# Batch 0's scores computed with tokens on partitions, raw weights loaded first, first weights used as two parts

## The chip, the cores and the metric

One core of a Trainium2 chip runs the kernel. The time is device microseconds; the kernel before takes 666.42 us, the median of 3 runs (665.63 to 666.83).

The engines are TensorE (PE, with its weight loads shown as PEld), VectorE (DVE), ScalarE (ACT), GpSimd (POOL, almost unused here), and SyncE (SP), whose queue issues all DMAs.

## The reference

Attention between 512 tokens and 32 states of each of 8 batches and 8 heads (dimension 64), in both directions, and then a feed-forward layer in which two products are multiplied elementwise.

```python
scores = scale * np.matmul(x, state.transpose(0, 1, 3, 2))
a = softmax(scores)                       # over the 32 states
xread = np.matmul(a, state)               # (B, H, 512, 64)
scores2 = scale * np.matmul(state, x.transpose(0, 1, 3, 2))
a2 = softmax(scores2)                     # over the 512 tokens
sread = np.matmul(a2, x)                  # (B, H, 32, 64)
x = concatenate([xread, sread], axis=2)   # to (4352, 512): heads side by side
return ((x @ w_a) * (x @ w_b)) @ w_out    # 512 -> 1536 -> 512
```

All arrays are float32. The weights come to the kernel as 64-bit floats in memory, seen as pairs of 32-bit words, and are rebuilt on the chip.

## The kernel before, in words

**Precision.** A float32 operand of the large products is kept as a high and a low part (`p_h`/`p_l`, `at_h`/`at_l`, `sd_h`/`sd_l` for batch 0's attention, `g_h`/`g_l`), and a product is three matmuls: high by high, high by low, low by high.

**Layer 1.** `x @ w` is not formed from xread. Since `xread @ w = a @ (state @ w)`, the kernel computes `state @ w` per batch and chunk of weights (`direct`, line 1298, for the first two chunks, from the float32 weights `wo6` to `wo9`), splits it into `p_h` and `p_l`, and multiplies by the attention weights `a`. The products land in the PSUM tiles `ab`; ACT and DVE multiply the two of them (`a_sb`), split the result (`g_h`, `g_l`), and layer 2 multiplies it by `w_out` (`wo0`, `wo1`, ...) into the PSUM tiles `acc`.

**The order of work.** The program only records its operations. `plan` (line 699) then sorts them, engine by engine, by estimated costs and by two tables of numbers, SHIFTS and RELEASES, and the loop at line 1798 issues them in that order. So nearly all instructions have the line 1798, each engine runs its list strictly in order, and a tile's name is what tells instructions apart. SP's DMAs are in one such list too; where one of them waits, those behind it wait.

**Start of the program.** `attend(0)` (line 1617) computes batch 0's attention in two halves of the heads, g = 0 and g = 1. For each half it computes the scores with states on the partitions (`scores`, 1111, tile `ms`), copies them to SBUF (`copied`, tile `p_raw`), turns them with four transposes so that tokens lie on the partitions (`scores_t`, 1138, tile `acc`), does the softmax over 32 states with DVE and ACT (`soft_t`, `exp`, `norm`, tile `s_p`), turns the result back (`back_t`, 1154) and splits it into `sd_h0` and `sd_l0`. The untransposed scores are also stored (`kept`), for the other direction later. `open_chunk(0)` (1674) loads the first chunk of weights in four raw blocks (`raw`, `raw`, `sd_h1`, `sd_l1` serve as rooms), each converted by `Whole` (960): ACT takes the upper words (`pre`, tile `t1`), DVE makes a rounded float32 from them (`wo6` and `wo7`) and a rest from the lower words (`t2`), and a last DVE addition joins the two. `direct` for batch 0 (`units[0].direct`, four calls of four matmuls, 64 rows by 32 columns of the array) follows each joined block.

80 matmuls on constants (`ab<-y`, line 894) run in the gaps of PE's list before its dense work.

After the start eight visits of one batch and two chunks each follow, then products over the remaining four chunks. The later batches' attention stands in between.

Of the kernel before, what the change touches and what calls it, by code (L numbers as in the profile page):

```python
# [10 lines left out]
F32 = mybir.dt.float32  # L11
# [9 lines left out]
P = 128  # L21
# [26 lines left out]
T0, PACE = 15e3, 1.12  # L48
STARTS = {}
# [246 lines left out]
class Engine:  # L296
# [557 lines left out]
def attn_moe(ctx, tc, xt, xn, sd, wl, w_out, out):  # L854
# [62 lines left out]
    class Conv:  # L917
# [6 lines left out]
        def load(self, place):  # L924
            self.raw = load64(self.src, place, self.runs)
            if not count[0]:
                u = rec.units[-1]
                u.serve, u.land, u.lat = u.serve + 1200, u.land + 900, u.lat + 2100
# [103 lines left out]
    def moving(c, f, g, hq):  # L1032
# [3 lines left out]
        if c:  # L1036
            return fw[c, g][rows, hq // 2]
# [803 lines left out]
```

## Time and profile before

| | before |
|---|---|
| median of 3 runs | 666.42 us |
| profiled execution | 665.46 us |
| its span | 663.3 us |
| DVE busy | 548.8 us, 83% |
| ACT busy | 383.0 us, 58% |
| DMA queue, share of 16 engines | 69.9% |

The times below come from the profiled execution. It is one of the executions of the program, and 0.96 us shorter than the median of the timed runs. A busy PE is not PE at its peak: an instruction's end is modelled, and two that overlap count once. What an engine waits for is inferred from its semaphores; the idle time stands in square brackets with the engine or DMA that ended it. In the timeline a row may hold several instructions of one kind. A float32 matmul (other than the split ones) shows as two in the trace.

### The profile page before, as it was taken

The numbers are of one execution on the slowest core, as the hardware profiler recorded it, in microseconds if no ns is written. First come the engines' busy times: TensorE is split into PE (matmuls) and PEld (weight loads), VectorE is DVE, ScalarE is ACT, GpSimd is POOL, SyncE is SP. The second block draws the span as 40 slices with busy tenths as digits, with TensorE's granted clock in tenths as the row PEclk, the third lists the DMA queues.
The fourth block names the chain that finished last, engine by engine and source line by source line (L and its number), as shares of the span: only waits on it lengthen the run. The fifth ranks groups of instructions, "written<-read, shape, count | busy, mean of one in ns | idle before, by whom it ended". The sixth has DMA issues, their size and how long they took to land.

```text
span 663.3 us, 12126 instructions
## 1 busy us (share of the span) xinstructions
PE 654.2 (99%) x4451; PEld 546.1 (82%) x4451; DVE 548.8 (83%) x1219; ACT 383.0 (58%) x707; POOL 0.7 (0%) x6
## 2 busy tenths in 40 slices
PE   7999999999999999999999999999999999999997
PEld 5566776776777778888888989898989989889996
DVE  5999989998877787878989978877777879877885
ACT  4677478699989976654545543534444444424442
POOL 0000000000000000000000000000000000000000
PEclk9999999999999999999999999999999999999999
DMA  8998579899989999866767764754426217168830
GB/s 304 354 366 332 222 253 344 301 317 356 351 300 393 339 327 351 328 189 198 257 235 219 246 232 124 249 168 159 155 101 169 102 48 223 65 182 188 233 97 33
DMA packets 75450, 155.98 MB, mean 235 GB/s; under 512 B 7040, under 2 KB 26240, under 8 KB 75392
## 3 DMA queue, kind: packets, MB, share of 16 engines
q1 hardware_dynamic: 75392, 155.22, 69.9%
q8 instruction: 35, 0.57, 0.4%
q14 instruction: 23, 0.19, 0.1%
HBM read 92.27 MB, written 62.91 MB: 234 GB/s over the span
## 4 chain that ended last, share of the span: by engine, by line
PE 93%; DVE 5%; issue 1%; DMA 0%; ACT 0%; DVEq 0%
PE ab L1798 44%; PE acc L1798 39%; PE ms L1798 10%; DVE t L1798 1%; DVE wo L1798 1%; DVE m L1798 1%; DVE s_p L1798 1%; DMA x<-xt 0%; DVE stg L1798 0%; DVE p_l L1798 0%; DVE x L1798 0%; ACT p_h L1798 0%; DVE a_sb L1798 0%; DVE u_c L1798 0%; DVE wq L1798 0%
## 5 line engine op out<-in xcount | busy, mean ns | idle before, releaser
L1798 PE MATMUL acc<-wo,g_h 128*128 128x256 f32 (+1 forms) x868 | 178.8, 316 | 0.3 <-DVE stg L1798 0.2
L1798 PEld LDWEIGHTS acc<-wo,g_h 128*128 128x128 f32 x868 | 135.4, 190 | 19.5 <-issue 3.4
L1798 PE MATMUL ab<-at_l,p_h 128*128 128x512 f32 x368 | 144.5, 393 | 0.0
L1798 PE MATMUL ab<-at_h,p_h 128*128 128x512 f32 x368 | 144.4, 397 | 0.0
L1798 PE MATMUL ab<-at_h,p_l 128*128 128x512 f32 x368 | 143.1, 391 | 0.0
L1798 PE MATMUL acc<-wo,g_l 128*128 128x256 f32 (+1 forms) x587 | 127.3, 308 | 0.2
L1798 PEld LDWEIGHTS acc<-wo,g_l 128*128 128x128 f32 x587 | 93.0, 190 | 11.5 <-issue 1.2
L1798 ACT CAST g_h<-a_sb 128x512 fp32r<-128x512 f32 (+1 forms) x104 | 64.0, 615 | 56.3 <-DVE a_sb L1798 26.6
L1798 PEld LDWEIGHTS ab<-at_h,p_h 128*128 128x128 f32 x368 | 69.1, 188 | 17.5 <-issue 2.9
L1798 PEld LDWEIGHTS ab<-at_h,p_l 128*128 128x128 f32 x368 | 69.1, 188 | 15.5 <-issue 0.8
L1798 PEld LDWEIGHTS ab<-at_l,p_h 128*128 128x128 f32 x368 | 69.3, 188 | 12.1 <-issue 0.8
L1798 DVE TENSOR_TENSOR g_h<-a_sb,g_h 128x512 fp32r<-128x512 f32 x68 | 46.7, 686 | 15.6 <-PE acc L1798 11.7
L1798 ACT COPY wq<-ab 128x512 f32<-128x512 f32 (+1 forms) x48 | 27.3, 569 | 43.5 <-PE ab L1798 43.3
L1798 DVE TENSOR_TENSOR wq<-ab,wq 128x512 f32<-128x512 f32 (+1 forms) x48 | 32.0, 666 | 21.9 <-PE ab L1798 18.9
L1798 ACT CAST p_h<-p_raw 128x1024 fp32r<-128x1024 f32 x32 | 33.7, 1054 | 21.7 <-PE ab L1798 20.5
L1798 DVE TENSOR_TENSOR p_l<-p_raw,p_h 128x1024 fp32r<-128x1024 f32 x32 | 39.0, 1218 | 1.5 <-ACT p_h L1798 1.4
L1798 DVE TENSOR_TENSOR stg<-acc,stg 128x256 f32<-128x256 f32 (+1 forms) x68 | 36.4, 552 | 3.6 <-PE acc L1798 2.6
L1798 ACT CAST g_l<-wq 128x384 fp32r<-128x384 f32 x46 | 23.6, 515 | 27.1 <-PE acc L1798 24.4
L1798 DVE TENSOR_TENSOR g_l<-wq,g_l 128x384 fp32r<-128x384 f32 x46 | 25.5, 555 | 14.5 <-PE acc L1798 9.8
L1798 ACT COPY p_raw<-ms 128x512 f32<-128x512 f32 x48 | 27.6, 591 | 10.7 <-PE ms L1798 8.5
L1798 DVE TENSOR_SCALAR t<-t 128x512 int32<-128x512 int32 x64 | 26.8, 420 | 5.3 <-ACT t L1798 5.0
L1798 DVE TENSOR_TENSOR a_sb<-ab,a_sb 128x512 f32<-128x512 f32 (+1 forms) x36 | 23.6, 657 | 6.7 <-PE ab L1798 5.3
(135 smaller groups left out, 1065.3 us busy)
## 6 DMA issues: line engine op xcount, KB each, us to landing
p_raw<-scr SPq DMA_DIRECT2D x32, 512.0 KB, 4.8
raw<-wl SPq DMA_DIRECT2D x20, 512.0 KB, 5.6
x<-xt SPq DMA_DIRECT2D x15, 576.0 KB, 7.1
out<-stg SPq DMA_DIRECT2D x33, 256.0 KB, 2.3
su<-wq SPq DMA_DIRECT2D x16, 512.0 KB, 5.8
scr<-sw_st SPq DMA_DIRECT2D x32, 256.0 KB, 4.6
scr<-p_raw SPq DMA_DIRECT2D x32, 256.0 KB, 4.8
x<-xn SPq DMA_DIRECT2D x16, 512.0 KB, 5.1
```

What stands on the lines that cost most here:

```text
L1798: getattr(obj, method)(*map(real, args), **{k: real(x) for k, x in kw.items()})
```

## The change

Four edits go together.

1. **Raw weights first.** The first raw block's load is issued before x's three loads (`head`), and its estimated landing in the planner is earlier.
2. **Scores straight.** For batch 0, `scores_t` no longer transposes. It multiplies with x as the stationary operand and the states as the moving one, so the scores come out with tokens on the partitions: for g = 0 eight matmuls with 64 columns moving, for g = 1 sixteen with 32. The scores with states on the partitions are still needed for `kept` and are computed after both halves.
3. **Two parts.** In the first chunk the rounded weight (`wo6`, `wo7`) and the rest (now in a `stg` tile instead of `t2`) are both multiplied and accumulated by `direct` for batch 0, and joined after it (`join`), for the other batches and for the stored copy.
4. **New tables.** SHIFTS and RELEASES have other numbers throughout, so that the whole order is sorted anew.

```diff
+XREL = 300.0
 SHIFTS = {
-    0: 961, 1: 522, 2: -345, 3: -1004, 4: 175, 5: 340, 6: 86993674, 7: 86992534, 8: -40, 9: 377, 10: -272, 11:
...
             if not count[0]:
                 u = rec.units[-1]
-                u.serve, u.land, u.lat = u.serve + 1200, u.land + 900, u.lat + 2100
+                u.serve, u.land, u.lat = u.serve + 600, u.land + 300, u.lat + 900
...
         def run(self):
             raw, t1 = self.raw, self.t1
-            o = self.parts()
-            t2 = proj.tile([P, 512], I32, name="t2")
+            o, t2 = self.parts()
...
-            nc.vector.tensor_tensor(out=f32(o), in0=f32(o), in1=f32(t2), op=ALU.add)
+            self.halves = o, f32(t2)
+
+        def join(self):
+            o, t2 = self.halves
+            nc.vector.tensor_tensor(out=f32(o), in0=f32(o), in1=t2, op=ALU.add)
...
-            return fw[c, i // 2][:, i % 2]
+            if c:
+                return fw[c, i // 2][:, i % 2], proj.tile([P, 512], I32, name="t2")
+            if i % 2 == 0:
+                rest_w[i // 2] = mlp.tile([P, 2, DM], F32, name="stg", bufs=4)
+            return fw[c, i // 2][:, i % 2], rest_w[i // 2][:, i % 2].bitcast(I32)
...
                     for h in range(2):
-                        nc.sync.dma_start(out=x[:, g, h], in_=xt[self.b, g, :, h])
+                        u = nc.sync.dma_start(out=x[:, g, h], in_=xt[self.b, g, :, h])
+                        u.rel = XREL
+                        u.touch.append(head.raw)
+                        u.acc.append((head.raw.tile, 0, False))
...
-            with rec.together(self.sp[g]):
+            with rec.together(self.sp[g]) as u:
                 for sb in range(4):
-                    nc.tensor.transpose(self.t[:, sb * P:(sb + 1) * P], self.s[g][:, sb * P:(sb + 1) * P], ident)
+                    x, o = slice(sb * P, (sb + 1) * P), self.t[:, sb * P:(sb + 1) * P]
+                    for h in range(2):
+                        if g == 0:
+                            nc.tensor.matmul(o.rearrange("p (i h n) -> p h i n", i=2, h=2)[:, h], lhsT=self.x[:, g, h, x],
+                                             rhs=self.st[:, g, h].rearrange("p (i n) -> p i n", i=2), start=True, stop=True)
+                        for hh in range(2) if g else ():
+                            j = place_of(g, 2 * h + hh)
+                            nc.tensor.matmul(o[:, j * NS:(j + 1) * NS], lhsT=self.x[:, g, h, x],
+                                             rhs=self.st[:, g, h, hh * NS:(hh + 1) * NS], start=True, stop=True)
...
-                            j, r = place_of(g, hq), moving(c, i, g, hq)
+                            j, parts = place_of(g, hq), (False, True) if psp else (False,)
...
+                            for k in parts:
+                                nc.tensor.matmul(ps[g][j * NS:(j + 1) * NS, x],
+                                                 lhsT=states_raw[hq % 2 * D:(hq % 2 + 1) * D, 2 * g + hq // 2, n],
+                                                 rhs=moving(c, i, g, hq, k), start=(i == fs[0] and not k),
+                                                 stop=(i == fs[-1] and k == parts[-1]))
...
         if a.wide:
             for g in range(NG):
-                a.scores(g)
-                a.copied(g)
                 a.scores_t(g, *where)
...
+            a.scores(0, 1)
+            for g in range(NG):
+                a.copied(g)
+                a.store(g)
             return
...
-            convert(whole(c, i), kind)
+            w = convert(whole(c, i) if c + i else head, kind)
             if c == 0:
                 units[0].direct(0, i // 2, i % 2, psp=ps_acc, tag="acc")
+            w.join()
...
+    head = whole(0, 0)
+    head.load(place(0, "early"))
+    count[0] += 1
```

How this moves instructions is seen in three places. The first is the start of PE's list, before, where `ms<-x` are the scores with states on the partitions and `acc<-ident,p_raw` their transposes:

```order
L1798 MATMUL ms<-x 32x512 x4
L1798 MATMUL ab<-y 128x256 x3
L1798 MATMUL acc<-ident,p_raw 128x128 x4
L1798 MATMUL ab<-y 128x256 x14
L1798 MATMUL ms<-x 32x512 x4
L1798 MATMUL ab<-y 128x256 x12
L1798 MATMUL acc<-ident,s_p 128x128 x4
L1798 MATMUL acc<-ident,p_raw 128x128 x4
```

and the same start of PE's list with the change, where `acc<-x` are the scores with tokens on the partitions:

```order
L1827 MATMUL ab<-y 128x256 x20
L1827 MATMUL acc<-x 128x2x32 x8
L1827 MATMUL ab<-y 128x256 x5
L1827 MATMUL ms<-x 32x512 x8
L1827 MATMUL ab<-y 128x256 x12
L1827 MATMUL acc<-ident,s_p 128x128 x4
L1827 MATMUL ab<-y 128x256
L1827 MATMUL acc<-x 128x32 x16
```

The transposes of scores are gone, 20 of the 80 warm-ups stand in front of all, and the scores of g = 1 come right behind the transposes of g = 0's result.

The second place is DVE's list from the second half's first reduction (g = 1) to its last multiplication, before (`wo7_210<-wo7_210,t2` are joins, `s_p_291` and `p_raw_267` belong to batch 1):

```order
L1798 TENSOR_REDUCE m1_238<-acc_196 128x16
L1798 TENSOR_TENSOR s_p_255<-acc_196,m1_238 128x512
L1798 TENSOR_SCALAR t2_257<-t1_234 128x512
L1798 TENSOR_SCALAR wo7_210<-t1_234 128x512
L1798 SCALAR_TENSOR_TENSOR t2_257<-sd_l1_144,t2_257 128x512
L1798 TENSOR_REDUCE m1_238<-s_p_255 128x16
L1798 TENSOR_TENSOR wo7_210<-wo7_210,t2_257 128x512
L1798 TENSOR_SCALAR m1_238<-m1_238 128x16
L1798 STREAM_TRANSPOSE s_p_291<-p_raw_267 128x512
L1798 RECIPROCAL m1_238<-m1_238 128x16
L1798 TENSOR_REDUCE m1_301<-s_p_291 128x16
L1798 TENSOR_TENSOR s_p_255<-s_p_255,m1_238 128x512
```

and with the change, behind the same first reduction and subtraction (`raw_143` is the first block of `w_out`, `sd_l1_152` the last raw block of the first chunk):

```order
L1827 TENSOR_SCALAR t2_292<-t1_265 128x512
L1827 TENSOR_SCALAR stg_228<-t1_223 128x512
L1827 TENSOR_SCALAR wo7_235<-t1_223 128x512
L1827 SCALAR_TENSOR_TENSOR stg_228<-sd_l1_152,stg_228 128x512
L1827 TENSOR_SCALAR t1_265<-t1_265 128x512
L1827 SCALAR_TENSOR_TENSOR t1_265<-raw_143,t1_265 128x512
L1827 TENSOR_REDUCE m1_286<-s_p_290 128x16
L1827 TENSOR_SCALAR raw_143<-t2_292 128x512
L1827 TENSOR_SCALAR m1_286<-m1_286 128x16
L1827 SCALAR_TENSOR_TENSOR wo0_295<-t1_265,raw_143 128x512
L1827 RECIPROCAL m1_286<-m1_286 128x16
L1827 TENSOR_TENSOR s_p_290<-s_p_290,m1_286 128x512
```

The joins and batch 1's operations have left this stretch, and five operations on `w_out` have come into it.

The third place is ACT's list around the exponential of g = 1, with the change (`t1_223` is the last raw block of the first chunk, `t1_265` and `t1_299` are the two first blocks of `w_out`, `s_p_290` the exponential):

```order
L1827 ACTIVATE t1_223<-sd_l1_152 128x512
L1827 ACTIVATE t1_265<-raw_143 128x512
L1827 CAST sd_l0_288<-acc_193 128x512
L1827 CAST wo0_295<-t2_292 128x512
L1827 ACTIVATE t1_299<-raw_232 128x512
L1827 ACTIVATE s_p_290<-s_p_290 128x512
```

Before, the exponential came right behind the conversion of the first chunk's last raw block, ahead of both blocks of `w_out`; now it stands behind both.

## Rows read from the trace of the kernel before

**Rows 1.** The page: span, and PE's busy time, share, instructions.

```profile
span 663.3 us, 12126 instructions
...
PE 654.2 (99%) x4451; PEld 546.1 (82%) x4451; DVE 548.8 (83%) x1219; ACT 383.0 (58%) x707; POOL 0.7 (0%) x6
```

**Rows 2.** Busy time by stage: stretch, length, then each engine's busy us.

```profile
0.00:26.00 26.00, 21.07 (x154) 14.79 (x155) 17.65 (x38) 11.62 (x21) 0.71 (x6) 1.00 0.93 323
```

**Rows 3.** Chain that ended last, 60 to 663.3 us, shares by line.

```profile
by line: PE ab L1798 46.4%; PE acc L1798 42.2%; PE ms L1798 9.2%; DVE stg L1798 0.3%; DVE p_l L1798 0.3%; DVE x L1798 0.2%; ACT p_h L1798 0.2%; issue 0.2%; DVE u_c L1798 0.1%; DVE wq L1798 0.1%; DVE xst L1798 0.1%; ACT u_c L1798 0.1%; DVEq
```

**Rows 4.** Timeline of DVE: start us, length us, engine, line, operation, tiles.

```profile
8.15 0.69 DVE L1798 TENSOR_REDUCE m<-acc 128x16 f32<-128x512 f32 x1 [8.15 <-PE acc L1798]
...
9.81 0.42 DVE L1798 TENSOR_SCALAR wo<-t 128x512 int32<-128x512 int32 x1
10.15 0.69 DVE L1798 SCALAR_TENSOR_TENSOR t<-raw,t 128x512 f32<-128x512 uint32 x1
...
10.75 0.68 DVE L1798 TENSOR_REDUCE m<-s_p 128x16 f32<-128x512 f32 x1
...
12.44 0.69 DVE L1798 TENSOR_TENSOR s_p<-s_p,m 128x512 f32<-128x512 f32 x1
...
16.79 0.69 DVE L1798 TENSOR_REDUCE m<-acc 128x16 f32<-128x512 f32 x1
...
22.01 1.28 DVE L1798 TENSOR_TENSOR s_p<-s_p,m 128x512 f32<-128x512 f32 x2
...
38.60 0.69 DVE L1798 TENSOR_TENSOR wo<-wo,t 128x512 f32<-128x512 f32 x1
```

**Rows 5.** Chain that ended last, 24 to 62 us: start us, us, what.

```profile
36.73 0.63 ACT g_h L1798
...
37.41 2.11 PE acc L1798 x8
```

**Rows 6.** Timeline of the first loads: an issue, and the end of PE's wait.

```profile
1.65 0.42 SPq L1798 DMA_DIRECT2D raw<-wl  x1
...
4.33 0.18 PEld L1798 LDWEIGHTS ms<-x 64*32 64x32 f32 x4 [0.50 <-DMA x<-xt]
```

**Rows 7.** Timeline of ACT: conversions of the raw blocks, with their waits.

```profile
8.56 0.67 ACT L1798 ACTIVATE t<-raw 128x512 f32<-128x512 f32 x1 [1.68 <-DMA raw<-wl]
...
11.73 0.67 ACT L1798 ACTIVATE t<-raw 128x512 f32<-128x512 f32 x1 [1.51 <-DMA raw<-wl]
...
15.92 0.68 ACT L1798 ACTIVATE t<-sd_l 128x512 f32<-128x512 f32 x1 [0.20 <-DMA sd_l<-wl]
```

**Rows 8.** Timeline of PE's weight loads, 128 by 128.

```profile
13.18 0.42 PEld L1798 LDWEIGHTS acc<-ident,s_p 128*128 128x128 f32 x4
...
25.84 0.19 PEld L1798 LDWEIGHTS ab<-sd_h,p_h 128*128 128x128 f32 x1 [0.95 <-ACT p_h L1798]
```

**Rows 9.** Timeline of PE: warm-ups, transposes, first weights, first dense matmul.

```profile
19.73 4.21 PE L1798 MATMUL ab<-y 128*128 128x256 f32 x33
...
23.78 0.60 PE L1798 MATMUL acc<-ident,s_p 128*128 128x128 f32 x4
...
24.30 1.07 PE L1798 MATMUL acc<-wo,xst 64*32 64x256 f32 x24
...
25.84 0.50 PE L1798 MATMUL ab<-sd_h,p_h 128*128 128x512 f32 x1 [0.47 <-ACT p_h L1798]
```

**Rows 10.** Chain that ended last, whole span: dense matmuls in a line.

```profile
89.47 2.72 PE ab L1798 x12
```

**Rows 11.** PE's groups by shape, 25.84 to 49.65 us: count, busy us, mean ns.

```profile
L1798 PE MATMUL ab<-sd_h,p_h 128*128 128x512 f32 x16 | 6.6, 412 | 0.5 <-ACT p_h L1798 0.5
...
L1798 PE MATMUL ms<-x 64*32 64x512 f32 x16 | 1.1, 601 | 0.0
...
L1798 PE MATMUL ab<-at_h,p_h 128*128 128x512 f32 x1 | 0.4, 389 | 0.0
```

**Rows 12.** DMA issues, 12.6 to 13 us: count, KB, us to landing.

```profile
raw<-w_out SPq DMA_DIRECT2D x1, 512.0 KB, 7.2
```

More of the change, by code (lines that the diff above doesn't have):

```diff
@@ L1015, in keep_w @@
                           in_=f32(w[c, hp]).rearrange("p a x -> p (a x)"))
-    fw = {}
+    fw, rest_w = {}, {}
     su_f = [dram.tile([2, P, 2, 2, 256], F32, name=f"sf{c}") for c in range(DIRECT)]
@@ L1030, in whole, with moving @@
         return Whole(wl[i // 2, :, 2 * (i % 2):2 * (i % 2) + 2, :], parts, 2)
-    def moving(c, f, g, hq):
+    def moving(c, f, g, hq, rest=False):
         rows = slice(hq % 2 * D, (hq % 2 + 1) * D)
+        if rest:
+            return rest_w[f][rows, g, hq // 2 * 256:(hq // 2 + 1) * 256]
         if c:
@@ L1114, in scores @@
                 self.s[g] = ps_ms.tile([P, 512], F32, name="ms")
-            with rec.together() as u:
+            self.pair = mlp.tile([P, NG, S], F32, name="p_raw")
+            with rec.together(self.pair) as u:
                 for hq in range(4):
@@ L1124, in scores @@
                 alone(u)
-            if self.b == 0 and gs == (0,):
-                late(u, 600)
         def copied(self, g):
-            if g == 0:
-                self.pair = mlp.tile([P, NG, S], F32, name="p_raw")
             self.e2[g] = self.pair[:, g]
@@ L1141, in scores_t @@
             self.sp[g] = att.tile([P, 16, 32], F32, name="s_p")
-            with rec.together(self.sp[g]):
+            with rec.together(self.sp[g]) as u:
                 for sb in range(4):
-                    nc.tensor.transpose(self.t[:, sb * P:(sb + 1) * P], self.s[g][:, sb * P:(sb + 1) * P], ident)
+                    x, o = slice(sb * P, (sb + 1) * P), self.t[:, sb * P:(sb + 1) * P]
[7 more added lines that the diff above has]
+                                             rhs=self.st[:, g, h, hh * NS:(hh + 1) * NS], start=True, stop=True)
+            if g == 0:
+                late(u, 600)
         def soft_t(self, g):
@@ L1308, in direct @@
                         for g in gs:
-                            j, r = place_of(g, hq), moving(c, i, g, hq)
+                            j, parts = place_of(g, hq), (False, True) if psp else (False,)
                             x = slice(256 * i, 256 * i + 256) if c == 0 else slice(0, 512)
-                            nc.tensor.matmul(ps[g][j * NS:(j + 1) * NS, x],
-                                             lhsT=states_raw[hq % 2 * D:(hq % 2 + 1) * D, 2 * g + hq // 2, n],
-                                             rhs=r, start=(i == fs[0]), stop=(i == fs[-1]))
+                            for k in parts:
[3 more added lines that the diff above has]
+                                                 stop=(i == fs[-1] and k == parts[-1]))
             if len(gs) == 1:
@@ L1602, in convert @@
     def convert(c, kind):
-        c.load(place(count[0], kind))
-        count[0] += 1
+        if c is not head:
+            c.load(place(count[0], kind))
+            count[0] += 1
         c.pre()
         c.run()
+        return c
     def flush():
@@ L1632, in attend @@
                 a.back_t(g, *where)
-                if a.keeps:
-                    a.store(g)
-                else:
-                    a.soft(g)
-                    a.out(g)
+            a.scores(0, 1)
+            for g in range(NG):
+                a.copied(g)
+                a.store(g)
             return
@@ L1702, in before @@
                  get=lambda c: get_w(c, ROOMS[c]))[what](x)
+    head = whole(0, 0)
+    head.load(place(0, "early"))
+    count[0] += 1
     prev = []
```

728 rows, old and new, of tables (RELEASES, SHIFTS) are left out of this document.

## The prediction

> **What bounds the kernel now.** I read the page first, then the busy time by stage, then the chain of waits, then the timeline of the first 30 us. The page shows TensorE busy for 654.2 of 663.3 us [rows 1]. The table by stage says where the other 9 us are: PE is busy 21.07 of the first 26 us [rows 2], and part of these 21 is warm-up matmuls that compute nothing; the rest, 4 us, is spread over 637. From 60 us on, the chain that ended last is over 97% matmuls (`ab`, `acc`, `ms`) [rows 3]. So an edit is worth what it does to two things: when the dense stream of PE begins, and how much PE has to do or wait from then on. Before that the chain runs through VectorE (DVE), from its first reduction at 8.15 us [rows 4] to what the cast at 36.73 waits for, behind which eight matmuls start at 37.41 [rows 5]. DVE therefore sets the pace of the start, and its first work waits for the scores of batch 0.
>
> **Loads.** The six opening transfers are the same, 512 KB of raw weights merely move ahead of the first x. Before, the two halves of x, 576 KB in all, had ended PE's waits by 4.33, and the first raw block, 512 KB issued at 1.65 [rows 6], let ScalarE (ACT) start its conversion at 8.56 [rows 7]. At the head of the queue raw can land as fast as x did (4.3 us), or take as long from its issue as it did, 6.9 us (7.6 us); I take 5.5. Both halves of x then have 512 KB more in front: not before 6.0, and not after 8.6, by which time the same bytes had landed before; I take 6.9, the lower half, since it is the raw block that came late. The second raw block has the same bytes in front as before and stays at 11.73 [rows 7], and so do those issued right behind it.
>
> **Batch 0, first half of the heads (g = 0).** Removed: score matmuls, an ACT copy and four transposes in front of DVE's first reduction. Added: 8 matmuls, in hardware 16 loads of 128x128 stationary x with 64 moving columns each. The trace has no f32 matmul of this shape. Four back-to-back loads of that size took 0.42 us, 0.105 each; one alone is recorded at 0.19 [rows 8]. I take 0.105, the row with several in a line, so 16 cost 1.7 us (3.0 by the other). First reduction: 6.9 + 1.8 = 8.7 us, with the semaphores 8.8, against 8.15 [rows 4]. What DVE gains is that the first raw block's three operations (0.34 + 0.34 + 0.60 by the distance of starts [rows 4]) now run earlier, at about 6.4 to 7.6, where it stood idle. From the first reduction to the end of the normalisation took 5.0 us, 8.15 to 13.1 [rows 4]; without the three conversions and the join in between, and with the wait for the exponential open instead, I count 0.7 + 0.7 + 0.7 (ACT) + 0.7 + 0.5 + 0.7 = 4.1 us: end at 12.9, 0.2 earlier.
>
> **Second half (g = 1).** PE takes its scores right behind the transposes of g = 0: 16 matmuls, 32 loads, 3.4 us at 0.105 (6.1 at 0.19). 12.9 + 0.6 + 3.4 = 16.9 us: DVE's second reduction starts where it did, 16.79 [rows 4]. From there to the end of its normalisation DVE had 5.2 us of other work and 0.7 of its own (22.69, the first of the two at 22.01). Now three of the joins and two operations of batch 1 in that stretch are gone, five conversions of `w_out` stand there instead (0.34, 0.34, 0.60, 0.34, 0.60), and their raw block reaches ACT behind the last raw weights, about 17.0, where these landed at 15.92 before [rows 7]. I come to 23.1 us. The transposes of that result started at 23.78 before, 1.1 us after they could, because 33 warm-ups stood in front [rows 9]; now the 36 warm-ups and 8 scores end near 23.2, so they start at 23.3: 0.5 us earlier.
>
> **First chunk as two parts.** Each of the 16 matmuls that make batch 0's first weights becomes two, 32 more hardware matmuls. Before, 24 of them took 1.07 us, 0.045 each [rows 9]. In front of the first dense matmul there are now 48 instead of 24: 1.1 us more; the 0.47 us that PE waited behind the old block for casts (25.37 to 25.84) covers part of it. 23.3 + 0.5 + 2.1 = 25.9: the dense stream begins where it did, at 25.84 [rows 9], give or take 0.4. The last quarter comes inside the dense stream: 16 instead of 8, +0.4 us. Four joins are not saved, only put later. All told DVE, ACT and SP execute what they did.
>
> **The stretch behind.** From 25.84 to 49.66 us PE had 79 matmuls of 512 columns (9 lines, 16 to 1 of each), 0.227 each by 12 in 2.72 us [rows 10], 17.9 us; four of 256 columns, 0.5; four blocks of small tiles, 0.6 to 1.1 us each, 3.6 without their tails [rows 11]. That is 22.0 of 23.8 us: 1.8 us are gaps. In this stretch PE first needs the second chunk's weights, which DVE finished late, behind batch 1's softmax and four joins. In the new order some 6 us of such work stand behind that point rather than in front, so these weights come near 34.6 us instead of 39.3, the end of the last join there [rows 4], and I expect 0.7 us of gaps, -1.1 (bounds: 0 and -1.8). The stores of the joined weights also leave the queue at this time, which makes room for loads; I count nothing for it.
>
> **Sum.** 0.0 + 0.4 - 1.1 = -0.7 us. The profiled execution took 665.46 us, which gives 664.8; it was 0.96 us under the median of the three runs, 666.42, so the forecast for the median is 665.7 us. Behind 60 us all orders are re-sorted, but PE has the same work and already waits for almost nothing; I put that at 0 with an uncertainty of 0.7.
>
> **Rivals.**
> *More gain.* The loads of g = 1 overlap with the short matmuls, 0.05 us each: the second reduction at 15.5 us. Next in line is the raw block of `w_out`, converted at about 17.7, so the normalisation ends at 22.2 and the dense stream starts 0.9 us earlier; with DVE that far ahead the gaps shrink by 1.8. -0.9 + 0.4 - 1.8 = -2.3: 664.1 us. For it: the two operands are read side by side elsewhere. Against: the 0.42 us for four loads were with short matmuls too.
> *Slower.* The 32 loads cost the recorded 0.19 us. PE then reaches the end of g = 1's scores at 19.6, DVE's second reduction waits 2.7 us, and all of the dense stream starts 2.0 us later (0.7 were slack against the `w_out` block); the gaps give back 0.4 less 0.4 for the extra parts: +2.0, 668.4 us. It decides from about 0.13 us per load. For it: the stationary side is now full-width x and the moving side 32 columns, the opposite of before.
> *Slower by ACT's order.* The exponential of g = 1 stands behind the conversion of the second `w_out` block. If that block takes the 7.2 us that the first such block took before [rows 12], it lands at 21.2 (its issue waits for DVE until about 14), not 18.9, and the exponential comes 2 us late: +1.3, 667.7 us. Against: some 1 MB less is queued in front of it than before.
> *No change.* Neighbours among the doubled matmuls now use the same rows and columns of the array, where before they alternated. If each pair runs after the other, the 48 take 1 us longer and eat the gain: 666.5 us. Against: a hardware matmul started every 0.045 us although each matmul already consists of two passes on one place [rows 9]. The Trainium skill (TensorE: Matmul & The Clock Gate, Part 3: Packing small matmuls — row/col tiling) says that a weight load overlaps with running matmuls only where its row group differs, which would speak for this rival; the two passes in the trace share theirs and do overlap, so I give it little.
>
> **How the numbers follow.** Forecast 45%, its own range 664.6 to 666.6; more gain 27%; slower by loads 11%; slower by ACT's order 7%; no change 10%. A measurement of this kernel tells some 0.2%, 1.3 us, from no change, so below 665.1 is faster and above 667.7 slower. Faster: 27% and a fifth of the forecast, 36%. Same: the rest of the forecast and the last rival, 46%. Slower: 18%. The range for 8 in 10 reaches from a little beyond the larger gain, 663.6, to 668.2 us.
>
> **What would show it.** In the new profile: ACT's first conversion near 5.5 us and DVE's first operation near 6.4; its first reduction at 8.8, its second at 16.9 (15.5 or 19.6 by the rivals on loads); the first `ab<-sd_h,p_h` at 25.9; the matmuls of the second chunk's weights before 36 us; the chain of waits free of DVE before 37 us; and no new waits on PE behind 60 us. I am wrong if the dense stream starts over 1 us off 25.9, or if the time is made or lost behind 60 us.

## The result and the profile after

The changed kernel takes 673.04 us (median of 4 runs, 672.03 to 674.27) against 666.62 for the kernel before in 4 runs: 1.010 times as long, 95% interval 1.008 to 1.012. That is 6.4 us slower, where 0.7 us faster was forecast, and beyond the range. The profiled execution took 672.88 us.

The page of the changed kernel, span and engines:

```profile
span 671.1 us, 12261 instructions
...
PE 660.3 (98%) x4523; PEld 552.6 (82%) x4523; DVE 551.3 (82%) x1219; ACT 381.8 (57%) x707; POOL 0.7 (0%) x6
```

DVE, ACT and POOL have as many instructions as in [rows 1]. PE has 72 more records: 48 of the straight scores and 32 of the second parts, less 8 transposes. PE is busy 6.1 us longer, and the span is 7.8 us longer.

Busy time by stage, columns as in [rows 2] (stretch, length; PE, PEld, DVE, ACT and POOL busy; PEclk; DMA share; GB/s). After:

```profile
0.00:26.00 26.00, 22.69 (x190) 20.28 (x198) 15.64 (x34) 9.96 (x17) 0.70 (x6) 0.93 0.82 281
26.00:60.00 34.00, 32.91 (x255) 20.97 (x240) 30.98 (x59) 22.98 (x47) 0.00 (x0) 1.00 0.98 368
160.00:300.00 140.00, 138.76 (x823) 107.27 (x820) 110.51 (x212) 110.11 (x200) 0.00 (x0) 1.00 0.93 324
```

and before, for the two stretches that [rows 2] don't hold:

```profile
26.00:60.00 34.00, 33.87 (x222) 22.40 (x223) 33.48 (x67) 24.64 (x49) 0.00 (x0) 1.00 1.01 375
160.00:300.00 140.00, 139.97 (x808) 111.50 (x807) 112.65 (x222) 111.62 (x203) 0.00 (x0) 1.00 0.92 322
```

Two things are new. The granted clock of the first stretch is 0.93, not 1.00. And PE, which had nearly no gaps from 26 us on, has them in both later stretches, 1.1 and 1.2 us.

PE's timeline up to the first dense matmul, after (start, length, engine, line, operation, tiles, count; in brackets what it waited for):

```profile
13.44 3.71 PE L1827 MATMUL acc<-x 128*128 128x32 f32 x32
...
18.82 5.13 PE L1827 MATMUL ab<-y 128*128 128x256 f32 x36
23.88 1.09 PE L1827 MATMUL ms<-x 64*32 64x512 f32 x16
24.90 0.66 PE L1827 MATMUL acc<-ident,s_p 128*128 128x128 f32 x4
25.48 0.71 PE L1827 MATMUL acc<-wo,xst 64*32 64x256 f32 x16
25.94 0.69 PE L1827 MATMUL acc<-stg,xst 64*32 64x256 f32 x16
26.97 0.50 PE L1827 MATMUL acc<-sd_h,y 128*128 128x512 f32 x1 [0.35 <-ACT sd_h L1827]
27.40 0.66 PE L1827 MATMUL acc<-wo,xst 64*32 64x256 f32 x8
...
28.42 0.50 PE L1827 MATMUL ab<-sd_h,p_h 128*128 128x512 f32 x1
```

The dense stream starts at 28.42, 2.6 us later than in [rows 9]; 25.9 was forecast. DVE's first reductions came about where they were expected, in its timeline after:

```profile
8.69 0.69 DVE L1827 TENSOR_REDUCE m<-acc 128x16 f32<-128x512 f32 x1 [1.57 <-PE acc L1827]
...
17.19 0.69 DVE L1827 TENSOR_REDUCE m<-acc 128x16 f32<-128x512 f32 x1 [1.94 <-PE acc L1827]
...
23.25 0.69 DVE L1827 TENSOR_TENSOR s_p<-s_p,m 128x512 f32<-128x512 f32 x1
```

What PE waited for from 60 us to the end (total us, times, longest), first before, then after:

```profile
PE acc L1798 <- DVE stg L1798: 0.2, 1, 0.2
```

```profile
PE ms L1827 <- ACT p_raw L1827: 1.0, 2, 0.5
PE ab L1827 <- ACT a_sb L1827: 0.6, 1, 0.6
PE acc L1827 <- DVE stg L1827: 0.4, 1, 0.4
PE ab L1827 <- DVE u_c L1827: 0.3, 1, 0.3
PE ab L1827 <- ACT wq L1827: 0.3, 1, 0.3
```

One wait of 0.2 us has become six of 2.6. Some time is also lost where no wait is listed, since the tail of the matmul in front covers it. Counted over the trace from 60 us on: 3 dense matmuls before start more than 0.25 us beyond their usual distance (0.227 us behind one of 512 columns, 0.120 behind one of 256), 0.9 us in all; after there are 9, 4.3 us.

### The profile page after: what moved, and what is told of

It is laid out like the page before. It is cut to its first block, busy times and chain, and to the rows that moved or that the text cites. A ratio compares the mean times of both kernels' runs of the same rounds, so it can differ in the third digit from the quotient of the medians.

```text
span 671.1 us, 12261 instructions
## 1 busy us (share of the span) xinstructions
PE 660.3 (98%) x4523; PEld 552.6 (82%) x4523; DVE 551.3 (82%) x1219; ACT 381.8 (57%) x707; POOL 0.7 (0%) x6
## 4 chain that ended last, share of the span: by engine, by line
PE 84%; DVE 6%; ACT 4%; DMA 4%; issue 1%; SPq 0%; DVEq 0%; ACTq 0%
PE ab L1827 41%; PE acc L1827 35%; PE ms L1827 8%; DMA scr<-p_raw 2%; ACT wq L1827 1%; DMA raw<-wl 1%; DVE m L1827 1%; DMA p_raw<-scr 1%; DVE a_sb L1827 1%; DVE t L1827 1%; DVE s_p L1827 1%; DVE p_l L1827 1%; DVE stg L1827 1%; DVE g_l L1827 0%; ACT p_raw L1827 0%
## 5 line engine op out<-in xcount | busy, mean ns | idle before, releaser
L1827 PE MATMUL acc<-wo,g_l 128*128 128x256 f32 (+1 forms) x587 | 130.1, 308 | 0.8 <-DVE stg L1827 0.4
L1827 PEld LDWEIGHTS ab<-at_l,p_h 128*128 128x128 f32 x368 | 69.3, 188 | 11.8 <-issue 0.4
L1827 DVE TENSOR_TENSOR wq<-ab,wq 128x512 f32<-128x512 f32 (+1 forms) x48 | 32.0, 666 | 12.6 <-PE ab L1827 12.2
L1827 DVE TENSOR_SCALAR t<-t 128x512 int32<-128x512 int32 x60 | 25.1, 418 | 5.8 <-ACT t L1827 5.4
```

What stands on the lines that cost most here:

```text
L1827: getattr(obj, method)(*map(real, args), **{k: real(x) for k, x in kw.items()})
```

## The experiments

Most test the order. The planner's tables can't be cut in pieces, so these kernels replace its result by a list of ranks, one for each recorded unit of work:

```diff
-    order, start = plan(rec.units, pools, T0)
+    order = follow(rec.units, pools, PLACES)
```

`follow` issues the unit of lowest rank whose data and whose buffers' former users stand ahead of it. With a kernel's own order as ranks it gives that order, row for row; with ranks from both kernels, a start from one and a rest from the other. Unless said otherwise a kernel is timed in 4 runs, beside 7 or more of the kernel before; after each time stand the ratio to the kernel before and its 95% interval.

**Start or rest.** Edit of the first: the changed code, ranks of after up to the first dense matmul, of before behind it. Of the second: before's code, the other way round.

> The changed kernel's four edits and its order of instructions up to its first dense matmul; behind that, the order of the kernel before. The profile of the changed kernel shows its first dense matmul 2.6 us later (28.42 against 25.84) and the stretch from there to the end 5.2 us longer (642.65 against 637.43). Theory 'two losses' (the start costs 2.6 us, the re-sorted rest about 4 to 5 us by itself): 669.2 us, first dense matmul near 28.4, the rest as long as before. Rival 'start alone' (the late start drags the rest along, whatever its order): about 673. Rival 'rest alone' (the 2.6 us at the start are given back behind): about 667.

> The converse: the kernel before without any of the four edits, its own order up to its first dense matmul, and behind it the order that the changed kernel has there. Theory 'two losses': first dense matmul near 25.8, total about 670.5 to 671.5. Rival 'start alone': 666.6, as before. Rival 'rest alone': 672 to 673.

The first took 671.64 us, 1.0089 (1.0067 to 1.0111), between the theory and the rival 'start alone'. PE waited only 0.5 us behind 60, but the dense stream came at 29.95, 1.5 later than in after with the same order in front: the granted clock was low there for 6.8 us and not 3.4 (below). The second took 676.53, 1.0154 (1.0135 to 1.0174), more than any of the three had it, and its seam spoils it; PE's timeline in it:

```profile
32.13 0.80 PE L1798 MATMUL ab<-sd_h,p_l 128*128 128x512 f32 x1 [5.27 <-ACT p_l L1798]
```

ACT had waited 3.1 us for raw weights ahead of this `p_l`, and the granted clock was 0.50 from 30.2 to 37.0 us. So I moved the seam to about 60 us, again with before's code and start and after's rest, and the reverse:

> The kernel before without any of the four edits and in its own order up to about 60 us; behind that, the changed kernel's order. The earlier run with the changed order straight behind the first dense matmul is disturbed at its seam (granted clock 0.50 to 0.60 at 30 to 32 us), so the seam is moved into the steady stream. Theory 'two losses': the first 60 us as before, TensorE about 4 us more idle behind them than before, total about 670.5. Rival 'start alone': 666.2.

> The changed kernel with its own order up to about 60 us; behind that, the order of the kernel before. Theory 'two losses': 673.0 less about 4 = 669. Rival 'start alone': 673. Rival 'rest alone': 666 to 667.

Old start, new rest: 670.12 us against 666.51, 1.0056 (1.0039 to 1.0072). The kernel before, with none of the first three edits, loses 3.6 us by after's order behind 60 us alone. Its dense stream starts at 25.94 and its clock is 1.00. PE's waits behind 60 us are 2.8 us in 7, nearly all of them after's kinds again; the first two:

```profile
PE ms L1798 <- ACT p_raw L1798: 0.9, 2, 0.5
PE ab L1798 <- ACT a_sb L1798: 0.6, 1, 0.6
...
```

By the count above it has 9 stops of 4.4 us in all, one of them (0.5) at the seam. That is 3.5 us more than before, as much as the loss. New start, old rest: 671.32, 1.0077 (1.0055 to 1.01); its two longest waits behind 60 us:

```profile
PE ab L1827 <- DVE a_sb L1827: 0.5, 1, 0.5
PE acc L1827 <- DVE wo L1827: 0.5, 1, 0.5
...
```

These lie at 63 to 66 us, at the seam, where the count finds 1.3 us of stops. So the start costs 2.9 us (673.04 less 670.12) to 4.8 (671.32 less 666.51, the seam included), and the rest 1.7 to 3.6. Each is a difference of two medians, whose intervals reach 1.1 to 1.5 us to either side, so the two ways don't contradict each other.

**What delays the start.** Four kernels with after's code and order and one or two edits. In the first the weights are joined ahead of `direct`, so that batch 0 uses one part:

```diff
-                            j, parts = place_of(g, hq), (False, True) if psp else (False,)
+                            j, parts = place_of(g, hq), (False,)
...
+            w.join()
             if c == 0:
                 units[0].direct(0, i // 2, i % 2, psp=ps_acc, tag="acc")
-            w.join()
```

> The changed kernel without the two accumulated parts: the first chunk's weight parts are added on VectorE in front of each direct product (0.68 us each by the changed kernel's rows), which then has half the matmuls (8 for 16 in the first group); the raw weights first, the straight scores and the order are kept. If the doubled matmuls lie on the path to the first dense matmul (TensorE waits only 0.35 us between 23.3 and 28.4 us of the changed kernel): first dense matmul near 27.4, total about 672.0. Rival (VectorE's additions come due there instead): first dense matmul 28.4 or later, total 673 to 674.

675.49 us, 1.0142 (1.0115 to 1.0168), more than the theory and the rival had it. PE's timeline in it:

```profile
26.36 0.66 PE L1827 MATMUL acc<-ident,s_p 128*128 128x128 f32 x4
...
29.24 0.50 PE L1827 MATMUL ab<-sd_h,p_h 128*128 128x512 f32 x1
```

From the transposes to the dense stream it is 2.88 us instead of 3.52: the second part costs 0.6, so it is not what makes after slow. Whether it pays is not settled by this run. The normalisation of g = 1 (the "norm" below) ends at 25.3, 1.4 later than after; a join of 0.6 stands in front of it, but the half clock also lasts longer here (15.8 to 22.7 us, below), and it stretched the scores to 4.59 us. And PE waited 2.5 us at 35.33 for `p_l`, since ACT waited 3.0 for raw weights; behind that wait the clock fell once more (0.57 from 36 to 40 us).

Nine of the 36 warm-ups left out:

```diff
         for i in order:
+            if i in range(60, 69):
+                continue
```

> The changed kernel with 27 in place of 36 warm-up matmuls ahead of the second half's transposes, nothing else moved. In the changed kernel the transposes began at 24.90, 0.96 us after VectorE had ended the normalisation (23.94), with the warm-ups and the next batch's scores in between. Theory (TensorE's queue is what is late there, since the warm-ups ran longer at the lower granted clock): transposes near 24.0, first dense matmul near 27.5, total 672.1. Rival (ScalarE's order ahead of the state's conversion is what is late): transposes earlier, first dense matmul still near 28.4, total 673.0.

673.35 us, 1.0118 (1.0079 to 1.0158): no gain. PE's timeline:

```profile
24.33 0.66 PE L1827 MATMUL acc<-ident,s_p 128*128 128x128 f32 x4
...
26.93 0.50 PE L1827 MATMUL acc<-sd_h,y 128*128 128x512 f32 x1 [0.88 <-ACT sd_h L1827]
```

The transposes start 0.6 us earlier, right behind the norm (24.27), and the wait for ACT's cast of their result grows by 0.5, so that the dense stream starts at 28.38, where it did. After's ACT timeline shows why:

```profile
25.07 0.59 ACT L1827 COPY p_raw<-ms 128x512 f32<-128x512 f32 x1 [3.80 <-PE ms L1827]
25.55 0.89 ACT L1827 ACTIVATE t<-sd_h 128x512 f32<-128x512 f32 x1
26.32 0.59 ACT L1827 CAST sd_h<-acc 128x512 fp32r<-128x512 f32 x1
```

ACT stands at the copy of the next batch's scores, 3.8 us idle, and runs that and a conversion ahead of the cast. The next kernel puts the cast first, with the fewer warm-ups; its ACT order, as a difference to after's:

```diff
-L1827 COPY p_raw<-ms 128x512
-L1827 ACTIVATE t_325<-sd_h_254 128x512
 L1827 CAST sd_h_217<-acc 128x512
+L1827 COPY p_raw<-ms 128x512
+L1827 ACTIVATE t_339<-sd_h_254 128x512
```

> The changed kernel with 27 in place of 36 warm-ups, as in the run before, and on ScalarE the state's conversion (sd_h<-acc) put ahead of the next batch's score copy (p_raw<-ms) and of one conversion of weights (t<-sd_h). With 27 warm-ups alone the transposes came at 24.33, 0.57 us earlier, and the first dense matmul at 28.38, as in the changed kernel. Theory (ScalarE's order is what is late at the first dense matmul): sd_h ends near 25.7 in place of 26.9, first dense matmul near 27.4, total 1 us less, 672.0 to 672.4. Rival (the doubled direct products fill TensorE's queue by themselves): first dense matmul at 28.0 or later, total 673.

671.63 us, 1.0078 (1.0062 to 1.0094), 1.4 less than after, though the two intervals overlap. PE's timeline:

```profile
26.23 0.50 PE L1827 MATMUL acc<-sd_h,y 128*128 128x512 f32 x1
...
27.75 0.50 PE L1827 MATMUL ab<-sd_h,p_h 128*128 128x512 f32 x1
```

The wait is gone and the dense stream starts 0.7 us earlier.

Last, the granted clock. Windows after, over the short score matmuls and behind them:

```profile
13.00:17.00 4.00, 4.00 (x38) 4.00 (x37) 2.26 (x6) 1.83 (x3) 0.00 (x0) 0.99 0.77 248
17.00:20.00 3.00, 3.00 (x14) 2.90 (x15) 2.77 (x6) 0.94 (x2) 0.00 (x0) 0.50 0.56 157
```

To see whether these matmuls bring the clock down, eight warm-ups are moved among them, one behind every four:

```diff
+            if 45 <= i < 53:
+                continue
+            for k, (obj, method, args, kw) in enumerate(rec.units[i].calls):
+                calls = [(obj, method, args, kw)] + (rec.units[45 + k // 2].calls if i == 101 and k % 2 else [])
```

> The changed kernel with 8 of the 36 warm-ups moved in among the second half's 32 short score matmuls, one behind every fourth. Theory (the granted clock falls to half because of what TensorE does in the short matmuls): granted clock 1.00 throughout the first 30 us, scores about 0.9 us longer (4.6 for 3.7), the warm-ups behind them 0.107 us each and not 0.142, transposes at 24.9 as before or 0.5 earlier, total 672 to 673 and the times of its runs closer together. Rival (the clock falls for another reason, such as the wait before the scores): granted clock 0.50 between 17 and 20 us as in the changed kernel, total 673 to 674.

673.42 us, 1.0104 (1.0083 to 1.0125). The window in it:

```profile
17.00:20.00 3.00, 3.00 (x27) 2.96 (x27) 2.00 (x5) 0.84 (x2) 0.00 (x0) 1.00 0.33 76
```

The clock stays at 1.00, as the theory had it, and nothing is won. The scores take longer with warm-ups among them, so the second reduction starts at 17.96 and the norm ends at 24.59, 0.65 later than after; batch 1's scores, next in PE's list, wait 0.35 us for their x; and the dense stream starts at 28.58. What the low clock costs in after is therefore not settled by this run.

**An earlier start.** Is a start before 26 us to be had from the edits? In six kernels the second half's scores come directly behind the first half's, with warm-ups among them, and batch 0's normalisation ahead of the `w_out` conversions; edit of all in PE's order (after, then the new one):

```diff
-L1827 MATMUL acc<-x 128x32 x16
-L1827 MATMUL ab<-y 128x256 x6
+L1827 MATMUL acc<-x 128x32 x2
+L1827 MATMUL ab<-y 128x256
+L1827 MATMUL acc<-x 128x32 x2
+L1827 MATMUL ab<-y 128x256
```

The first pair has 53 warm-ups, with after's rest and with before's:

> The changed kernel's edits with its start put in another order by hand: the second half's 32 short score matmuls directly behind the first half's (no longer behind the first half's transposes, which wait for VectorE's normalisation), with 8 warm-ups and those transposes among them; the store's scores behind them; VectorE normalises the second half before it converts the fourth block of weights and w_out; ScalarE converts state and pieces first; 53 warm-ups in all in place of 80; the changed kernel's order behind. In the changed kernel those scores began at 13.44 though their input was there before 9.23, VectorE waited 1.94 us for them, and w_out's conversions stood in front of the second normalisation (17.92 to 23.94). Theory (the start was late by its order, not by its edits): second reduction near 14, normalisation over near 18, first dense matmul near 21, and the rest's loss of about 3.6 us stays: 667 to 669. Rival (VectorE's conversions and not TensorE's order limit the first 60 us): first dense matmul near 21 to 22, but TensorE waits behind it as much longer, total 671 to 673.

> The same start, and behind its first dense matmuls the order of the kernel before. Theory: the early start and the old rest together beat the kernel before: 664 to 666. Rival (VectorE's conversions limit the first 60 us): 667 to 669, with TensorE waiting between 21 and 60 us.

678.13 us, 1.0182 (1.0161 to 1.0203), and 677.72, 1.0167 (1.0152 to 1.0183). The dense stream started at 25.13 and 25.43, and PE stood still for 3.9 us up to 34.77 and for 5.8 up to 35.91, both for ACT's `p_l`. SP's queue shows what made it late in the first:

```profile
21.18 0.34 SPq L1827 DMA_DIRECT2D kept<-p_raw  x1
...
23.07 0.38 SPq L1827 DMA_DIRECT2D sd_h<-wl  x1
```

A store that waits for its source, `p_raw` from ACT (11.8 us), stands in front of the second chunk's raw weights. In the second kernel the granted clock also fell in the dense stream, where PE stood still, and stayed low behind it:

```profile
39.00:40.00 1.00, 1.00 (x5) 0.81 (x4) 0.57 (x1) 0.00 (x0) 0.00 (x0) 0.50 1.00 401
```

It was 0.50 from 31.6 to 41.8 us, with PE busy for 5.85 of them; at half speed that is an estimated 2.9 us lost besides the wait. The second and third pair have 61 warm-ups, and the second these loads first:

> The start of the two runs before with its faults taken out. There ScalarE wrote the warm-ups' operand only behind the first conversion, so that TensorE began at 5.99 in place of 2.39; and on SyncE's queue a store (kept<-p_raw, which waits for ScalarE's copies) stood in front of the loads of w_out, of the next batch's x and of weights (21.18 to 24.78), behind which TensorE waited 3.9 us for p_l. Now the operand comes first, the loads stand ahead of the store, and ScalarE converts the pieces ahead of weights that still have to land. The changed kernel's order behind. Theory (the start was late by its order, not by its edits): first dense matmul near 21, total 667 to 669. Rival (the supply from VectorE and the loads limits the first 60 us): first dense matmul near 21, TensorE waiting 4 us or more between there and 60 us, total 671 to 673.

> The same start, and behind its first dense matmuls the order of the kernel before. Theory: 663 to 665, faster than the kernel before. Rival (supply): 667 to 669, TensorE waiting between the first dense matmul and 60 us as much as it began earlier.

685.04, 1.0278 (1.0262 to 1.0295), and 679.61, 1.0193 (1.0176 to 1.021). The dense stream starts at 21.45 in the first of them, and then PE's timeline and SP's queue show:

```profile
42.20 3.35 PE L1827 MATMUL ms<-x 64*32 64x512 f32 x16 [13.92 <-DMA x<-xt]
```

```profile
24.37 0.33 SPq L1827 DMA_DIRECT2D e<-kept  x1
...
35.40 0.92 SPq L1827 DMA_DIRECT2D x<-xt  x2
```

A read of `kept` waits 5.8 us at the head of the queue; behind it come weights and a store that waits 3.4 us for ACT, and only then the next x. The third pair has the loads of x ahead of such stores and reads:

> The early start once more, with the order of loads set by when each is wanted. In the last run TensorE began its dense matmuls at 21.85 and then stood 13.1 us for the next batch's x, whose load I had put behind a read of a stored tile (e<-kept, issued at 24.73, waiting for a store from 18.5) and behind weights. Now on SyncE's queue the loads of weights and x come first, the read of the stored tile comes after them, the second batch's scores stand earlier on TensorE (they free the one buffer of x) and the third batch's later; ScalarE converts w_out between the two p_l. Old order behind. Theory (the start was late by its order, not by its edits): first dense matmul near 21.5, no wait above 1 us behind it, 663 to 665. Rival (the supply of loaded and converted weights limits): waits of 4 us or more in sum before 60 us, 667 to 670.

> The same start with the changed kernel's order behind. Theory: 667 to 669. Rival (supply): 671 to 674.

672.54, 1.0109 (1.0077 to 1.014), and 677.04, 1.0154 (1.0132 to 1.0177). The trace of the first is of its longest execution, 676.58 us; the other three took 672.15 to 672.60, and what they waited for isn't known. In the traces the dense streams start at 24.61 and 21.39; PE's longest wait in the first:

```profile
38.05 0.79 PE L1827 MATMUL ab<-sd_h,p_h 128*128 128x512 f32 x1 [4.33 <-DVE a_sb L1827]
```

The second waits 2.4 us up to 30.64 (`a_sb`) and 2.5 up to 40.92 (`g_h`). All six took longer than both their theory and their rival. In each trace what came early was lost again within the first 50 us, to such waits and to the half clock that came with them. My orders by hand have faults of their own, so this doesn't show that no order could keep it.

**Single edits of the kernel before.** Its own order with nine of the 33 warm-ups left out and one cast moved behind `p_h`:

```diff
         for i in order:
+            if i in range(60, 69):
+                continue
```

> The kernel before, none of the four edits: 24 warm-ups in place of 33 ahead of the second half's transposes (in its trace VectorE's first of the two products s_p<-s_p,m at 22.01 is over near 22.7 and the transposes begin at 23.78), and on ScalarE one conversion of w_out (wo<-t, 0.62 us) behind the pieces p_h, for the first of which TensorE waits 0.47 us. Theory (the start limits by TensorE's queue and ScalarE's order alone): transposes near 22.8, first dense matmul near 24.5 in place of 25.84, total 665.2. Rival (what follows has its own due time, VectorE's conversions): first dense matmul near 24.5 and the gain lost before 60 us, total 666.5.

666.13 us against 666.34, 0.9997 (0.9988 to 1.0006), 11 runs: the same. The dense stream starts at 25.07, 0.8 us earlier, and PE's timeline has the answer 7 us later:

```profile
32.22 0.50 PE L1798 MATMUL ab<-sd_h,p_h 128*128 128x512 f32 x1 [0.88 <-DVE a_sb L1798]
```

The same order with the first raw weights loaded and converted ahead of x; edit in SP's order:

```diff
+L1798 DMA raw<-wl 128x1024
 L1798 DMA x<-xt 128x576 x2
+L1798 DMA x<-xt 128x1152
 L1798 DMA raw<-wl 128x1024
-L1798 DMA x<-xt 128x1152
-L1798 DMA raw<-wl 128x1024
```

and then the same once more with the two edits of the kernel before it, the nine warm-ups and the cast:

> The kernel before with one edit alone, in its own order otherwise: the first block of raw weights is loaded ahead of the first batch's x, and its conversion (ScalarE's first, VectorE's four) stands ahead of the first reduction. In the kernel before, VectorE's first operation begins at 8.15 and these four take about 2.2 us of it (9.48, 9.81, 10.15, 11.35); x, which then lands later, has to pass ms, p_raw and transposes first. Theory (the edit itself costs nothing, the re-sorted order did): first reduction near 9.0 to 9.4, VectorE abreast of the kernel before or up to 1 us ahead at the second reduction (16.79), first dense matmul 25.5 to 25.9, total 665.8 to 666.5. Rival (the edit itself costs the 3 us of the start): first dense matmul 27 or later, total 668 or more.

> The same with the two edits of the run with 24 warm-ups and w_out's conversion behind p_h. That run began its dense matmuls 0.77 us earlier than the kernel before and lost it again to one wait for VectorE (a_sb, 0.88 us at 32.2). Theory (VectorE ahead by the conversion done early keeps what the early start gains): no such wait, total 664.8 to 665.5, faster than the kernel before. Rival (other work of the first 40 us is due at its own time): again a wait near 32 us, total 666.

667.4 us, 1.0013 (1.0004 to 1.0022), and 667.68, 1.0013 (1.0004 to 1.0023), 11 runs each. DVE's first reduction in the first:

```profile
10.76 0.69 DVE L1798 TENSOR_REDUCE m<-acc 128x16 f32<-128x512 f32 x1 [2.83 <-PE acc L1798]
```

PE's first scores on x start at 6.30, 2.6 us later than before, and the first reduction is 2.6 later than in [rows 4]. Of that 0.75 is left at the dense stream (26.59) and 0.9 in the time: alone, the first edit costs a little. In the last kernel PE waits 0.96 us at 33.50 for DVE's `a_sb`, so its earlier point is given back too.

## Why the prediction was wrong

**Two terms of the sum failed, and either alone makes the kernel slower.** Both signs that the prediction named for being wrong came: a dense stream over 1 us off 25.9, and time lost behind 60 us. One failed term is the last: "Behind 60 us all orders are re-sorted, but PE has the same work and already waits for almost nothing; I put that at 0 with an uncertainty of 0.7." It measured +3.6 us, 1.7 by the other way of taking it apart. That before has hardly a wait there shows that its order fits, and no more. Another order of the same work could win little more than the 0.9 us of stops that are left (delays under 0.25 us are not counted), and lose much more, so the uncertainty should have been on one side. In the kernel with the old start and the new rest the instructions are the same as before, and the usual distances of 0.227 and 0.120 us are the same in all three; what grew is stops. One of after's waits, ACT's timeline in front of it and PE's line:

```profile
209.19 0.62 ACT L1827 CAST wq<-t 64x512 fp32r<-64x512 f32 x1
209.84 0.59 ACT L1827 COPY p_raw<-ms 128x512 f32<-128x512 f32 x1
```

```profile
210.48 0.50 PE L1827 MATMUL ms<-wq,sd_h 128*128 128x512 f32 x1 [0.54 <-ACT p_raw L1827]
```

PE needs the `ms` buffer that the copy empties, and ACT runs two other operations first, this cast and a copy at 208.54, in the order of its list. No table of busy time shows that beforehand.

The other failed term is the start with the stretch to 60 us, "0.0 + 0.4 - 1.1 = -0.7 us". It measured +2.9 to +4.8.

**The start of the dense stream**, forecast at 25.9, came at 28.42. By its steps:
- Loads and both score products were right: first reduction 8.69 (8.8 forecast), 32 loads of x in 3.71 us (3.4), second reduction 17.19 (16.9). The rivals at 15.5 and 19.6 fall. Two small sums in the prediction are off: the six terms of g = 0's normalisation add up to 4.0 us, not 4.1 (it took 4.02), and "no change" comes to 666.7 by its own price of 1 us, not 666.5.
- The norm of g = 1 ended at 23.94, not 23.1: 0.8 us, of which 0.3 was there at the second reduction.
- "The 36 warm-ups and 8 scores end near 23.2": they end at 24.9. The 36 take 5.13 us, 0.142 each, where 33 took 4.21, 0.128 each [rows 9], part of them at half clock; batch 1's scores then stand ahead of the transposes. 1.6 us late, of which the norm explains half; taking nine warm-ups away moved the transposes by 0.6, to where the norm ended.
- The doubled products were right: 32 in 1.1 us (25.48 to the end of the next row, 26.6) and 16 in 1.0, 2.2 with rounding beside the 2.1 forecast. That is 0.045 us each, as before [rows 9], so the rival that priced pairs at 1 us more falls. The Trainium skill's rule on weight loads, which was set beside it (TensorE: Matmul & The Clock Gate, Part 3: Packing small matmuls — row/col tiling), shows no price here.
- "23.3 + 0.5 + 2.1" leaves out ACT's cast between transposes and products and the small matmuls at 26.97: from transposes to dense stream it took 3.52 us, not 2.6. I had looked at ACT's order only around the exponential. The rival "slower by ACT's order" had the right kind of mechanism, but at another place; putting the cast first, with fewer warm-ups, brought the dense stream 0.7 us forward.
- The prediction has no term for the clock, which was 1.00 throughout [rows 2]. In after it was low from 16.9 to 20.3 us. With the same order in front and the clock low for 6.8 us, the kernel with the new start and the old rest started its dense stream 1.5 us later still. How much of after's own 2.6 us is the clock's isn't shown.

**The gaps from 26 to 60 us**, forecast 1.1 us smaller, grew by 1.0: PE was busy 32.91 of 34 us, against 33.87. Of after's 1.1, 0.35 is the wait in front of the dense stream, which the start has counted already, and the rest is one wait on PE:

```profile
33.21 0.73 PE L1827 MATMUL ab<-sd_h,p_l 128*128 128x512 f32 x2 [0.75 <-ACT p_l L1827]
```

The matmuls of the second chunk's weights, forecast before 36 us, came at 39.02, hardly ahead of the 39.45 of before, so the premise of a DVE that is far ahead failed. The row of before also shows 0.13 us where I had reckoned 1.8 from counts and durations: what I took for gaps was nearly all covered by matmuls' tails, and the view of busy time by stage, taken over this stretch, would have said how little it shows to win.

How much of the start's 2.9 to 4.8 us belongs to each edit stays open: raw weights first cost 0.9 by themselves, in before's order; the two parts cost 0.6 on PE, less what they save on DVE; the scores' own share was never run apart from the order. Whether the first three edits could keep a gain under an order fitted to them stays open too.

## What to carry to other kernels

Where an order of in-order engines was fitted to a kernel, a new order of the same work is an edit of its own with a one-sided risk, here 1.7 to 3.6 us against the 0.7 that the four edits were after: price it, and read the waits behind the edited place as well as at it. A start that comes earlier is worth only what the next operand keeps up with; find the next operand that is late (here `a_sb` or `p_l`, 7 us on) before counting a gain.

## What the runs showed of the hardware

The granted clock fell to 0.50, the 1.2 GHz level, while PE was recorded as busy without a gap: 4.00 of 4.00 us from 13 to 17 us in the changed kernel, most of it the short score matmuls. The Trainium skill (TensorE: Matmul & The Clock Gate, Part 1: The HAM clock gate) gives the low level to an idle or cold TensorE; the row in front of the fall shows neither. With after's start the clock was back by 20.3 us; in the kernel with one part per weight the fall lasted longer. A window of after, behind the one at 0.50 shown above, and then one of that kernel:

```profile
20.30:22.00 1.70, 1.70 (x17) 1.70 (x16) 1.64 (x4) 0.97 (x2) 0.00 (x0) 1.00 1.04 356
```

```profile
16.20:22.70 6.50, 6.50 (x31) 6.40 (x31) 5.03 (x11) 2.34 (x5) 0.00 (x0) 0.50 0.62 208
```

The traces of all six kernels that run the 32 short score matmuls of the second half in one row show this fall, between 15.8 and 18.5 us. Of the seven with warm-ups among them, six stayed at 1.00 there, and one fell all the same, the first of the third pair. Its trace, and that of the second of the third pair, which has the same order up to the dense stream:

```profile
13.00:19.00 6.00, 6.00 (x34) 4.01 (x35) 4.27 (x9) 2.04 (x4) 0.00 (x0) 0.50 0.36 132
```

```profile
16.00:17.00 1.00, 1.00 (x11) 1.00 (x10) 1.00 (x3) 1.00 (x3) 0.00 (x0) 1.00 0.88 238
```

The clock's price shows in this pair: their first reductions lie 0.1 us apart (8.76 and 8.66), but the first, with 0.50 from 13.0 to 19.9 us, starts its dense stream at 24.61 and the second at 21.39, 3.2 us earlier. So the warm-ups go with fewer falls, but the mixture alone doesn't decide it, and what does was not found.

The clock also fell in the dense stream, in eight kernels by hand, during or just behind a wait of PE; these waits were 2.4 to 13.9 us long. The longest fall was that of the second of the second pair, 0.50 from 31.3 to 48.3 us, where PE had stood still up to 41.49 for the next x. A late operand there cost its wait and a stretch at half speed behind it.
